# A first part in another order, and two attention spots joined to their neighbours at the end of the second block

## The chip, the core and the metric

The kernel runs on one core of one Trainium2 chip. The metric is the device time of one execution in microseconds (us). Five engines work side by side, each through its own queue in order: TensorE (PE, with PEld for its weight loads), VectorE (DVE), ScalarE (ACT), GpSimd (POOL), and SyncE (SP), which issues the DMAs.

## The reference, cut to what matters

```
out = attention(q, k, v, mem_k, mem_v)     # 4 x 8 heads x 768 x 64; chunks of 32 queries,
                                           # 64 keys each: 16 left, 32 own, 8 right, 8 memory
x   = out as 3072 tokens x 512
h   = x @ w_in                             # 512 -> 2048
g   = s * relu(h)**2 + b
x   = g @ w_out                            # 2048 -> 512
logits = x @ phi                           # 32 slots
slot_in  = softmax(logits over tokens).T @ x
slot_out = relu(slot_in @ w1[e]) @ w2[e]   # 8 experts, 4 slots each
return softmax(logits over slots) @ slot_out
```

## The kernel before

The 3072 tokens are six blocks of 512. Attention is cut into units: one unit is one pair of heads of one block, so a block has four. A unit has three spots on TensorE, with work of other engines between them:

- `att_qk` (line 220): 16 score matmuls of 64x64 into one bank. Then the softmax: on DVE two memsets of masked columns, a maximum (234), a subtraction (235); on ACT the exponential (239); on DVE the sum (247), an added epsilon (248), a reciprocal (249); and a scaling (253), on DVE or, in the first part, on POOL.
- `att_turn` (263): four transposes. `att_half` copies the two halves of the result to a tile `pb`, on ACT (273) or on DVE (275).
- `att_pvmm` (285): 16 value matmuls of 64x64. `att_copy` brings the result to SBUF on ACT (292 or 294), `att_low` forms its low part on DVE (308).

Every large product is done in three matmuls with high and low parts of both operands ("split": the high part by ACT, the low part by DVE or POOL).

Blocks 0 and 1 run in steps n = 0 to 31, sixteen of d_ff for each block. A step has twelve matmuls for h (`mm_h`, 377), then `make_r` (381, ACT), `make_t` (385, DVE), `make_high` (388, ACT), `make_low` (392, DVE), and, one step later, twelve matmuls for y (`mm_y`, 407). The weights arrive as 64-bit words in halves, and each half goes through four operations before it can be used: `w_clamp` (d in the list below, 326), `w_low` (h, 335), `w_high` (e, 330) and `w_end` (E, 340).

The first part, with block 0's attention and all of block 0's steps, follows a list of tokens, `FIRST`: a letter for an operation and a number for the unit, step or half. It sets the order on every engine: B `att_qk`, a maximum and subtraction, b exponential, f sum and reciprocal, j scaling on POOL, U `att_turn`, p and C the two copies to `pb`, V `att_pvmm`, u `att_copy`, X `att_low`, I and i the split of w_in, H and M `mm_h`, z dummy matmuls.

Attention of later units is spread over the steps by the table `bg`. Steps 28 to 31 (`hand_step`) and all that follows up to the tail are in an order written out by hand, which ACT, DVE and POOL keep; PE and SP keep the written order throughout. In a hand step, `tasks` holds the attention spots of the step: a value spot stands ahead of `make_g` (385 to 392), a score or transpose spot behind it.

Blocks 2 and 3 follow in `first_super`, eight rounds p. A round makes seven products (`prod`, 737) into four banks. At its head, bank A (`bank[4]`) takes product a11; ACT copies it out (808, to y0n); product s1 goes to bank C (`bank[6]`); then s2 is added onto what is in A, so PE waits for the copy 808 first. ACT copies C out (826, to y1n), and s4 is added onto C, so PE waits for copy 826. In round 0 both copies stand on ACT's queue behind work of step 31: the split of the operands t2, t3, t4 (651 on ACT, 655 and 665 on DVE) and of the weights w14n, w15n (728 on ACT, 729 on POOL).

Unit 17 is the second of block 4's units; in the kernel before, its scores stand in round 0 between s2 and s4, and its softmax behind s3.

Of the kernel before, what the change touches and what calls it, by code (L numbers as in the profile page):

```python
# [25 lines left out]
KG = 40  # L26
KW = CB * KG + 24
FIRST = (
# [25 lines left out]
def tile_attention_moe_softmoe(  # L54
# [158 lines left out]
    def att_qk(u, b):  # L213
        S = b.rearrange("p (t n) -> p t n", t=8)
        qt, kt = qv(u), kv(u)
        for i in range(4):
            for z in range(2):
                for par in range(2):
                    c = 4 * i + 2 * par + z
                    pe.matmul(S[64 * par:64 * par + 64, 2 * i + z, :], lhsT=qt[:, c].rearrange("p h n -> p (h n)"), rhs=kt[:, KG * c:KG * c + 64],  # L220
                              start=True, stop=True)
# [19 lines left out]
    def att_exp(u, b):  # L241
        att_top(u, b)
        att_e(u)
# [11 lines left out]
    def att_norm(u, last=None):  # L255
        att_sum(u)
        att_mul(u, last or dve)
# [11 lines left out]
    def att_half(u, b, z, fast=True):  # L269
        src = b.rearrange("p (i a h n) -> p i a h n", i=4, a=2, h=2)[64 * z:64 * z + 64]  # L270
        dst = pbv(u)[64 * z:64 * z + 64, :, :, :, z, :]
        if fast:
            act.activation(out=dst, in_=src, func=AF.Copy)  # L273
        else:
            dve.tensor_copy(dst, src)
# [46 lines left out]

    def w_clamp(k):
        hv = half_at[k].rearrange("p (n w) -> p n w", w=2)[:, :, 1]
        eng = dve if k in (0, 1) else pool
        eng.tensor_scalar(out=hv, in0=hv, scalar1=-EXP_TOP, scalar2=EXP_TOP, op0=ALU.max, op1=ALU.min)  # L326

    def w_high(k):
# [243 lines left out]
    for u in range(2 * NHP, 4 * NHP + 1):  # L572
        n0 = NF - 4 + 2 * (u - 2 * NHP)
        bg[n0].append(("qk", u))
        bg[n0 + 2].append(("tr", u))
        bg[n0 + (4 if u < 4 * NHP - 2 else 3)].append(("pv", u))
    for step, task in ((3, "log"), (3, "ytr0"), (5, "etr"), (5, "ytr1"), (7, "ytr2"), (7, "ytr3"), (7, "csoft"), (9, "slot")):
        bg[NF + step].append((task, 0))
    for n, tasks in bg.items():
# [5 lines left out]
    def att_next(a):  # L585
        if a + 2 < NB * NHP:
            load_q(a + 2)
            load_k(a + 2)
# [172 lines left out]
    def first_super(pending):  # L761
# [41 lines left out]
        for p in range(NPR):  # L803
            c11 = hl(ch[0])[:, p % 2]
            more = p + 1 < NPR
            A, D = yq[0], yq[3]
            prod(A, "a11", "b11", p)
            act.activation(out=c11, in_=A, func=AF.Copy)
            if p == 0:
                x_split("t4", 0, 1)  # L810
            if p:
                att_place(4 * NHP + p, D)
                finish(p - 1)
            if p == 1:
                w_split(2, 1)
                evac_spare(yp)
            if p == 5:
                run_bg("csoft", jr)
            if more:
                w_sums(p + 1)  # L820
            w_split(3, p)
            wi_load(p + 2)
            if not more:
                t2_load(0)
            prod(C, "s1", "t1", p)
            act.activation(out=c22, in_=C, func=AF.Copy)
            w_prep(0, p + 1)
            if not more:
                prep(0)
                x_split("b11", 1, 0)  # L830
                x_split("b11", 1, 1)
            prod(A, "s2", "t2", p, False)
            act.activation(out=c12, in_=A, func=AF.Copy)
            w_prep(1, p + 1)
            if not more:
                t2_load(1)
            if p:
                run_bg("pv", 4 * NHP + p, B)
            if more:
                att_qk(4 * NHP + p + 1, D)  # L840
                att_next(4 * NHP + p + 1)
                if p:
                    att_exp(4 * NHP + p + 1, D)
                    att_norm(4 * NHP + p + 1)
            pending.pop(0)()
            if p:
                next_load(p, 0)
            prod(C, "s4", "b22", p, False)
            dve.tensor_tensor(out=c12, in0=C, in1=c12, op=ALU.add)
            if not more:  # L850
                x_sum("t1", 1, 0)
                x_sum("t1", 1, 1)
            prod(A, "s3", "t3", p, False)
            dve.tensor_tensor(out=c22, in0=A, in1=c22, op=ALU.add)  # L854
            if p == 0:
                att_exp(4 * NHP + 1, D)
                att_norm(4 * NHP + 1)

            def square2():
                relu(r2, ch[1])  # L860
                times(cur[G2[p]], ch[1], r2)
                if p:
                    w_prep(2, p + 1)

            if p:
                square2()
            if not more:
                t2_load(4)
                prep(1)
                x_split("t1", 1, 0)  # L870
                x_split("t1", 1, 1)
            late = lambda: None
            for t in routing.get(p, ()):
                if t == "log":
                    late = y_logits(jr, D)
                else:
                    run_bg(t, jr, B if t in ("ytr0", "ytr1", "ytr3") else D)
            pending.pop(0)()
            if p:
                next_load(p, 1)  # L880
            else:
                ws_load(R[3], 1)
            if not more:
                t2_load(6)
                t2_load(7)
            prod(A, "a22", "t4", p, False)
            relu(t21, A)
            times(t21, A, t21)
            late()
            prod(B, "a12", "b21", p)  # L890
            if not more:
                t2_load(5)
            dve.tensor_tensor(out=c11, in0=B, in1=c11, op=ALU.add)
            g_high(t21, G[1])
            relu(t11, c11)
            g_low(t21, G[1])
            times(t11, c11, t11)
            if p == 0:
                square2()
            if more:  # L900
                att_turn(4 * NHP + p + 1, D)
            pending.append(lambda p=p: mm_job(yp, cur[R[(2 * p) % 4]], G[1], p == 0, False))
            pending.append(lambda p=p: mm_job(yp, cur[R[(2 * p + 1) % 4]], G[0], False, p == NPR - 1))
# [327 lines left out]
    with tc.manual_schedule(engines={mybir.EngineType.PE, mybir.EngineType.SP}):  # L1231
# [28 lines left out]
        def took(u, b=None):  # L1260
# [33 lines left out]
            "f": att_sum,  # L1294
            "j": lambda u: att_mul(u, pool),
            "p": lambda u: att_half(u, sbk[u], 0),
            "C": lambda u: att_half(u, sbk[u], 1, u in (0,)),
            "u": lambda u: att_copy(u, sbk[u]),
            "X": lambda u: att_low(u, sbk[u]),
            "Z": w_store,  # L1300
# [32 lines left out]
        def hand_step(n):  # L1333
            m = n - (NSTEP - 4)
            if m == 0:
                split_wi(n + 1)
                wi_load(0)
                wi_load(1)
                ws_load(R[0], NPR, True)
                ws_load(R[1], 0, True)  # L1340
            split_wo(n)
            sp.dma_start(out=DWS[n % NF], in_=WO[n % 2])
            mm_h(n, (0, 1, 2, 3))
            if m == 3:
                w_split(1, 0)
            make_r(n)
            tasks = [lambda t=t, a=a: run_bg(t, a, bank[7] if n == NSTEP - 1 else HB[(n + 1) % 2] if t == "pv" else mbank())
                     for t, a in bg[n]]
            if bg[n][0][0] == "pv":
                tasks.pop(0)()  # L1350
            make_g(n)
            if n + 2 < NSTEP:
                split_wi(n + 2)
            for t in tasks:
                t()
            mm_y(n - 1)
            if m == 0:
                x_sum("t1", 0, 1, pool)
            elif m == 1:
                x_split("t1", 0, 1)  # L1360
            elif m == 2:
                w_sums(0)
                x_sum("t2", 0, 1)
                x_sum("t3", 0, 1)
                x_split("b22", 0, 1)
                w_split(0, 0)
            else:
                x_split("t2", 0, 1)
                x_split("t3", 0, 1)
                x_sum("t4", 0, 1)  # L1370
                w_split(2, 0)
                ws_load(R[2], NPR + 1)
# [258 lines left out]
```

## Time and profile before

| what | us |
|---|---|
| median of three timed runs | 650.23 (649.72 to 650.28) |
| the profiled execution | 649.8 |
| its span, first to last instruction | 648.0 |
| PE busy | 636.5 (98%) |
| DVE, ACT, POOL busy | 441.0, 354.8, 281.2 |

Times in the trace count from the start of the span; the profiled execution lasted 1.8 us longer than its span. PE's mean granted clock was 0.997 of full speed. An engine's busy share is a mean over the whole span; what matters here is the order in which things end in two stretches, the first 26 us and the 12 us from 230 on.

### The profile page before, as it was taken

How to read it: one execution, taken by the hardware profiler on the slowest of the kernel's cores; microseconds unless marked ns; L12 is line 12 of the kernel's file. 1: busy time of each engine (PE TensorE's matmuls, PEld its weight loads, DVE VectorE, ACT ScalarE, POOL GpSimd, SP SyncE). 2: the span in 40 equal slices, each digit the busy share in tenths (PEclk: the TensorE clock that was granted, in tenths of full speed). 3: DMA queues.
4: the chain of work that ended last, by engine and by line, in shares of the span. 5: the costliest groups of instructions: out<-in, count | busy, mean ns of one | idle time of the engine just before them, and what ended most of it. 6: DMA issues, size and time to landing. Idle time of an engine off the chain costs nothing.

```text
span 648.0 us, 12886 instructions
## 1 busy us (share of the span) xinstructions
PE 636.5 (98%) x4965; PEld 511.6 (79%) x4965; DVE 441.0 (68%) x716; ACT 354.8 (55%) x640; POOL 281.2 (43%) x227
## 2 busy tenths in 40 slices
PE   8999999999999999999999999999999999999995
PEld 7788888888878888888788887888887888886384
DVE  6999989666864678656566587616766889676233
ACT  5898887655554556554354555425654456554232
POOL 5897856343333584643534103454455515320000
PEclk9999999999999999999999999999999999999998
DMA  8998854577746755978754687469999789999998
GB/s 331 408 405 306 307 184 171 170 274 252 262 168 212 286 200 211 332 263 297 285 192 180 218 294 227 183 196 379 333 344 323 243 291 334 331 379 409 406 408 323
DMA packets 59821, 183.33 MB, mean 283 GB/s; under 512 B 6640, under 2 KB 7920, under 8 KB 59760
## 3 DMA queue, kind: packets, MB, share of 16 engines
q1 hardware_dynamic: 59760, 182.51, 77.5%
q8 instruction: 39, 0.64, 0.4%
q14 instruction: 22, 0.18, 0.1%
HBM read 136.35 MB, written 46.14 MB: 282 GB/s over the span
## 4 chain that ended last, share of the span: by engine, by line
PE 96%; DVE 2%; ACT 0%; issue 0%; DVEq 0%; POOL 0%; POOLq 0%
PE bank L407 28%; PE bank L737 24%; PE bank L377 13%; PE bank L995 12%; PE bank L285 3%; PE bank L220 3%; PE bank L1486 2%; PE bank L1445 2%; PE bank L459 2%; PE bank L263 2%; PE bank L433 1%; PE bank L475 1%; PE bank L1515 1%; PE bank L1245 1%; PE bank L513 0%
## 5 line engine op out<-in xcount | busy, mean ns | idle before, releaser
L407 PE MATMUL bank<-g,wo 128*128 128x512 f32 x528 | 130.0, 395 | 0.0
L407 PEld LDWEIGHTS bank<-g,wo 128*128 128x128 f32 x528 | 96.9, 188 | 21.7 <-ACT wi L347 0.8
L377 PE MATMUL bank<-x,wi 128*128 128x512 f32 x384 | 92.8, 390 | 0.0
L377 PEld LDWEIGHTS bank<-x,wi 128*128 128x128 f32 x384 | 71.8, 188 | 15.3 <-DVE x L308 0.4
L385 DVE SCALAR_TENSOR_TENSOR rt<-bank,cons,rt 128x512 f32<-128x512 f32 x32 | 23.8, 745 | 29.1 <-ACT rt L381 28.9
L326 POOL TENSOR_SCALAR sp<-sp 128x512 f32<-128x512 f32 x20 | 43.0, 2174 | 0.0
L366 POOL TENSOR_TENSOR wo<-w,wo 128x512 fp32r<-128x512 f32 x16 | 21.9, 1367 | 45.3 <-ACT wo L362 32.5
L729 POOL TENSOR_TENSOR w14n<-sp6n,w14n 128x512 fp32r<-128x512 f32 x8 | 14.5, 1815 | 46.9 <-ACT w14n L728 46.9
L351 POOL TENSOR_TENSOR wi<-w,wi 128x512 fp32r<-128x512 f32 x17 | 22.4, 1318 | 24.8 <-ACT wi L347 21.3
L347 ACT ACTIVATE wi<-w 128x512 fp32r<-128x512 f32 x32 | 20.1, 629 | 19.9 <-PE bank L377 15.0
L392 DVE SCALAR_TENSOR_TENSOR g<-rt,cons,g 128x512 fp32r<-128x512 f32 x32 | 25.6, 799 | 6.2 <-ACT g L388 5.9
L362 ACT ACTIVATE wo<-w 128x512 fp32r<-128x512 f32 x32 | 20.1, 627 | 16.4 <-PE bank L407 9.0
L285 PEld LDWEIGHTS bank<-pb,v 128*64 128x64 f32 x704 | 22.2, 138 | 8.0 <-issue 2.5
L388 ACT ACTIVATE g<-rt,cons 128x512 fp32r<-128x512 f32 x32 | 23.1, 720 | 9.0 <-DVE rt L385 8.5
L239 ACT ACTIVATE ep<-ep 128x512 f32<-128x512 f32 x22 | 13.9, 632 | 23.1 <-DVE ep L235 23.0
L285 PE MATMUL bank<-pb,v 128*64 128x64 f32 x704 | 25.1, 225 | 0.8 <-ACT pb L273 0.5
L220 PE MATMUL bank<-k,q 128*64 128x64 f32 x704 | 24.8, 226 | 0.0
L752 ACT ACTIVATE rt1n<-y1n 128x1024 f32<-128x1024 f32 x8 | 8.5, 1058 | 29.0 <-DVE y1n L854 29.0
L220 PEld LDWEIGHTS bank<-k,q 128*64 128x64 f32 x704 | 22.9, 141 | 1.4 <-issue 1.3
L381 ACT ACTIVATE rt<-bank 128x512 f32<-128x512 f32 x32 | 18.7, 583 | 6.3 <-PE bank L377 6.1
L985 POOL TENSOR_TENSOR k0n<-sp5n,k0n 128x512 fp32r<-128x512 f32 x6 | 8.2, 1360 | 30.4 <-ACT k0n L984 30.3
L247 DVE TENSOR_REDUCE ast<-ep 128x8 f32<-128x512 f32 x22 | 15.0, 681 | 8.6 <-ACT ep L239 8.2
(696 smaller groups left out, 1742.4 us busy)
## 6 DMA issues: line engine op xcount, KB each, us to landing
v<-vd SPq DMA_DIRECT2D x22, 512.0 KB, 5.1
sp<-wd SPq DMA_DIRECT2D x22, 512.0 KB, 9.3
q<-qd SPq DMA_DIRECT2D x20, 512.0 KB, 7.3
dws<-wo SPq DMA_DIRECT2D x16, 512.0 KB, 6.3
k<-kd SPq DMA_DIRECT2D x22, 332.0 KB, 7.0
wo<-dws SPq DMA_DIRECT2D x12, 512.0 KB, 4.5
dwi<-w SPq DMA_DIRECT2D x16, 256.0 KB, 6.5
dwr<-w SPq DMA_DIRECT2D x16, 256.0 KB, 6.3
```

The source lines that it names most:

```text
L220: pe.matmul(S[64 * par:64 * par + 64, 2 * i + z, :], lhsT=qt[:, c].rearrange("p h n -> p (h n)"), rhs=kt[:, KG * c:KG * c + 64], start=Tru ...
L285: pe.matmul(b[64 * h:64 * h + 64, 64 * m:64 * m + 64], lhsT=vt[:, m, h, :], rhs=pb[:, m // 2, m % 2, h].rearrange("p z n -> p (z n)"), sta ...
L326: eng.tensor_scalar(out=hv, in0=hv, scalar1=-EXP_TOP, scalar2=EXP_TOP, op0=ALU.max, op1=ALU.min)
L351: (dve if n < NF and n not in (0,) else pool).tensor_tensor(out=r32(t[:, 1]), in0=raw, in1=t[:, 0], op=ALU.subtract)
L366: (dve if n < NF else pool).tensor_tensor(out=r32(t[:, :, 1]), in0=raw, in1=t[:, :, 0], op=ALU.subtract)
L377: pe.matmul(HB[n % 2], lhsT=r32(w[:, a, kt, :]), rhs=r32(x[:, b]), start=(kt == 0 and i == 0), stop=(kt == 3 and i == 2))
L385: dve.scalar_tensor_tensor(out=t, in0=HB[n % 2], scalar=s_col, in1=r, op0=ALU.mult, op1=ALU.mult)
L388: act.activation(out=r32(hl(G[n % 2])[:, 0]), in_=hl(RT[n % 2])[:, 1], func=AF.Identity, bias=b_col)
L392: dve.scalar_tensor_tensor(out=r32(g[:, 1]), in0=t, scalar=b_col, in1=g[:, 0], op0=ALU.add, op1=ALU.subtract)
L407: pe.matmul(yb[dt], lhsT=r32(w[:, dt // 2, a, dt % 2 * 128:dt % 2 * 128 + 128]), rhs=r32(g[:, b]), start=(first and i == 0), stop=(last an ...
L737: pe.matmul(b, lhsT=r32(wv[:, a, kt, :]), rhs=r32(xv[:, c]), start=(first and kt == 0 and i == 0), stop=(kt == 1 and i == 2), skip_group_c ...
L995: pe.matmul(banks[d], lhsT=r32(w[:, a, d * 128:d * 128 + 128]), rhs=r32(g[:, b]), start=(first and i == 0), stop=(last and i == 2), skip_g ...
```

## The change

It has four parts.

1. The head of `FIRST` is rewritten. Units 0 to 3 keep their sequence on PE, but of the copies to `pb`, C1 and C3 go from DVE to ACT; `w_low` and `w_high` of weight half 0 go to other places on ACT; tiles for weight halves are handed out in another order further on.
2. `w_clamp` of half 0 goes from DVE to POOL.
3. The value spot of unit 14 goes from step 27 to step 28.
4. The scores of unit 17 and their whole softmax go from round 0 of `first_super` to step 31, behind the value spot of unit 16 and ahead of `make_g(31)`.

```diff
-    "q0 k0 q1 k1 K0 q2 k2 q3 k3 v0 w1 v1 v2 v3 w3 z8 S0 s0 B0 S1 s1 a0 B1 S2 s2 b0 B2 a1 S3 s3 f0 b1 B3 "
...
+    "q0 k0 q1 k1 K0 q2 k2 q3 k3 v0 w1 v1 v2 v3 w3 z8 S0 s0 S1 s1 B0 a0 B1 S2 s2 a1 z2 B2 b0 f0 S3 s3 a2 "
+    "b1 B3 f1 j0 k4 w1 a3 K1 z4 b2 h0 q4 w2 U0 d0 p0 z5 C0 e0 b3 j1 f2 V0 U1 u0 p1 j2 f3 C1 U2 p2 E0 C2 "
...
     def w_clamp(k):
...
-        eng = dve if k in (0, 1) else pool
+        eng = dve if k in (1,) else pool
...
-        bg[n0 + (4 if u < 4 * NHP - 2 else 3)].append(("pv", u))
+        bg[n0 + (4 if u < 4 * NHP - 1 else 3)].append(("pv", u))
...
             if p:
                 run_bg("pv", 4 * NHP + p, B)
-            if more:
-                att_qk(4 * NHP + p + 1, D)
-                att_next(4 * NHP + p + 1)
-                if p:
-                    att_exp(4 * NHP + p + 1, D)
-                    att_norm(4 * NHP + p + 1)
+            if more and p:
+                run_bg("qk", 4 * NHP + p + 1, D)
...
-            if p == 0:
-                att_exp(4 * NHP + 1, D)
-                att_norm(4 * NHP + 1)
...
-            "C": lambda u: att_half(u, sbk[u], 1, u in (0,)),
+            "C": lambda u: att_half(u, sbk[u], 1, u in (0, 1, 3)),
...
             if bg[n][0][0] == "pv":
                 tasks.pop(0)()
+            if m == 3:
+                run_bg("qk", 4 * NHP + 1, bank[6])
             make_g(n)
```

The first place is PE at the end of block 1: the difference in steps 28 and 31 and in round 0 (285 value matmuls, 220 scores, 263 transposes, 407 y, 737 products).

```order
 L377 MATMUL bank_195<-x_93,wi_83 128x512 x3
 L377 MATMUL bank_195<-x_94,wi_83 128x512 x3
+L285 MATMUL bank_196<-pb_105,v_103 64x64 x16
 L220 MATMUL bank_197<-k_101,q_99 64x64 x16
 L263 MATMUL bank_198<-cons,ep 128x128 x4
@@ -549,4 +549,5 @@
 L377 MATMUL bank_196<-x_94,wi_84 128x512 x3
 L285 MATMUL bank_198<-pb_105,v_103 64x64 x16
+L220 MATMUL bank_197<-k_102,q_100 64x64 x16
 L407 MATMUL bank_191<-g_95,wo_85 128x512
```

Unit 14's values now stand directly ahead of unit 16's scores, and unit 17's scores directly behind unit 16's values.

The second place is ACT's queue at the same point, after the change: from `make_r(31)` (381) to the copy of bank C (826).

```order
L381 ACTIVATE rt_98<-bank_196 128x512
L294 ACTIVATE x00n<-bank_198 128x512
L239 ACTIVATE ep<-ep 128x512
L388 ACTIVATE g_96<-rt_98,cons 128x512
L651 ACTIVATE w11n<-x01n 128x512
L651 ACTIVATE w12n<-x01n 128x512
L728 ACTIVATE w14n<-sp6n 128x512
L808 ACTIVATE y0n<-bank_195 128x512
L651 ACTIVATE w13n<-x01n 128x512
L728 ACTIVATE w15n<-sp4n 128x512
L826 ACTIVATE y1n<-bank_197 128x512
```

Before, the row of line 239 stood much later, behind the copies 808, 826 and 833; the others stood in this same order.

The third place is DVE's queue there, after the change: from the low part of t3's first half (655, w10n) on.

```order
L655 TENSOR_TENSOR w10n<-x03n,w10n 128x512
L233 MEMSET bank_197 64x8
L231 MEMSET bank_197 64x16
L234 TENSOR_REDUCE ast_188<-bank_197 128x8
L235 TENSOR_TENSOR ep<-bank_197,ast_188 128x512
L247 TENSOR_REDUCE ast_188<-ep 128x8
L248 TENSOR_SCALAR ast_188<-ast_188 128x8
L249 RECIPROCAL ast_188<-ast_188 128x8
L253 TENSOR_TENSOR ep<-ep,ast_188 128x512
L385 SCALAR_TENSOR_TENSOR rt_98<-bank_196,cons,rt_98 128x512
L392 SCALAR_TENSOR_TENSOR g_96<-rt_98,cons,g_96 128x512
```

Before, 385 came directly behind w10n, and the eight rows of the softmax stood further on, behind the two additions onto y1n (849, 854).

## Rows read from the trace of the kernel before

**Rows 1.** The page: busy time and share of each engine.

```profile
PE 636.5 (98%) x4965; PEld 511.6 (79%) x4965; DVE 441.0 (68%) x716; ACT 354.8 (55%) x640; POOL 281.2 (43%) x227
```

**Rows 2.** Waits of PE, total, times, longest in us; the longest of nine.

```profile
PE bank L1245 <- POOL w L1241: 1.3, 1, 1.3
```

**Rows 3.** The chain of waits: start, us, engine, line, instructions.

```profile
195.55 1.08 PE bank L285 x32
196.64 0.93 PE bank L220 x32
...
231.25 2.94 PE bank L407 x12
234.19 4.08 PE bank L737 x18
238.27 1.08 PE bank L220 x32
239.36 2.95 PE bank L737 x12
242.30 2.72 PE bank L407 x12
```

**Rows 4.** DVE's timeline, 230 to 248 us: start, us, line, operation.

```profile
231.64 0.75 DVE L385 SCALAR_TENSOR_TENSOR rt<-bank,cons,rt 128x512 f32<-128x512 f32 x1
...
235.06 1.78 DVE L665 TENSOR_TENSOR x01n<-x03n,x01n 128x512 f32<-128x512 f32 x1
...
243.10 0.07 DVE L233 MEMSET bank<- 64x8 f32 x1
...
247.23 0.74 DVE L755 SCALAR_TENSOR_TENSOR rt0n<-bank,cons,rt0n 128x512 f32<-128x512 f32 x1
```

**Rows 5.** ACT's timeline, 230 to 241 us.

```profile
232.43 0.72 ACT L388 ACTIVATE g<-rt,cons 128x512 fp32r<-128x512 f32 x1 [0.53 <-DVE rt L385]
...
234.10 0.62 ACT L728 ACTIVATE w14n<-sp6n 128x512 fp32r<-128x512 f32 x1
235.59 0.60 ACT L808 ACTIVATE y0n<-bank 128x512 f32<-128x512 f32 x1 [0.88 <-PE bank L737]
...
237.93 0.58 ACT L826 ACTIVATE y1n<-bank 128x512 f32<-128x512 f32 x1
```

**Rows 6.** DVE's timeline, 12 to 26 us.

```profile
15.97 0.38 DVE L326 TENSOR_SCALAR sp<-sp 128x512 f32<-128x512 f32 x1
...
17.55 0.69 DVE L275 COPY pb<-bank 64x512 f32<-64x512 f32 x1
18.28 0.98 DVE L340 SCALAR_TENSOR_TENSOR w<-sp 128x512 uint32<-128x512 uint32 x1
...
24.51 0.68 DVE L308 TENSOR_TENSOR x<-bank,x 128x512 fp32r<-128x512 f32 x1
```

**Rows 7.** POOL's timeline, 10 to 40 us.

```profile
13.64 1.04 POOL L253 TENSOR_TENSOR ep<-ep,ast 128x512 f32<-128x512 f32 x1 [1.49 <-ACT pb L273]
16.20 1.06 POOL L253 TENSOR_TENSOR rt<-rt,ast 128x512 f32<-128x512 f32 x1 [1.51 <-DVE ast L249]
...
21.25 10.99 POOL L326 TENSOR_SCALAR sp<-sp 128x512 f32<-128x512 f32 x5
```

**Rows 8.** PE's timeline, 12 to 32 us.

```profile
17.31 0.66 PE L263 MATMUL bank<-cons,rt 128*128 128x128 f32 x4 [0.18 <-POOL rt L253]
18.30 1.15 PE L285 MATMUL bank<-pb,v 128*64 128x64 f32 x32 [0.33 <-DVE pb L275]
...
22.35 1.15 PE L285 MATMUL bank<-pb,yt 128*64 128x64 f32 x32 [0.26 <-DVE pb L275]
```

**Rows 9.** Instructions on the tile of weight halves, 5 to 20 us: issues, and landing times.

```profile
L320 SPq DMA_DIRECT2D sp<-wd x7: 327/328/436, 5.5 to 18.8; - x7
...
DMA to landing us min/median/max: 7.0/10.3/11.4
```

**Rows 10.** Stretches: busy us of each engine, granted clock, DMA share, GB/s.

```profile
644.00:648.00 4.00, 0.00 (x0) 0.00 (x0) 0.00 (x0) 0.00 (x0) 0.00 (x0) 0.58 0.63 252
```

5 rows, old and new, of the table FIRST are left out of this document.

## Prediction

> **What bounds the kernel now.** I read the page first, then PE's waits, then the chain that ended last, then the timelines of the two stretches that the change touches. The page shows PE busy for 636.5 us [rows 1]; the list of waits has nine for PE, together 5.5 us, the longest 1.3 us at the very start [rows 2], and all of them lie in the first 23 us or behind 596 us. Between these the kernel costs what PE's instructions cost. So a gain has to be PE work that vanishes or a start that comes earlier, and a wait that the change makes inside this stretch is paid in full: nothing later can absorb it. DVE, ACT and POOL are ahead of PE there, and the question for each edit is by how much.
>
> **Two joins.** A lone spot of 64x64 matmuls takes 1.08 us, and the group of twelve wide matmuls behind it takes 2.95 instead of 2.72: 1.08 + 0.23 = 1.31 us. A spot directly behind another one takes 0.93 [rows 3]. Unit 17's scores stood alone (at 238.27) and will stand behind unit 16's values: 1.31 - 0.93 = 0.38 saved. Unit 14's values stood alone with the same two durations, and will stand ahead of unit 16's scores, which then lose the 0.15 of a first spot, while the 0.23 behind the values goes: 0.38 again. Together 0.75 us.
>
> **What unit 17's softmax does in step 31.** This is the part that decides. All times here are those of the trace of before, with the y group of step 30 as the anchor. That group began at 231.25 [rows 3]; now unit 17's scores stand ahead of it, so they end at 231.25 + 0.93 = 232.18. DVE's queue has the softmax next, ahead of line 385. In round 0 the same eight operations took from 243.10 to 247.23, with the exponential of ACT in the middle: 4.13 us [rows 4]. So 385, which started at 231.64, starts at 232.18 + 4.13 = 236.31, which is 4.67 later. Behind it on ACT stand, in order, 388, the high parts of w11n and w12n, w14n, and only then the copy 808 of bank A. From the start of 385 the row of 388 begins 0.79 later and that of w14n ends 3.08 later [rows 4, 5]; 808 would follow at once and takes 0.60, and since neighbours on ACT overlap by about 0.1, it ends 3.6 after 385: at 239.9. Before, it ended at 236.19 and waited for PE, not PE for it.
>
> PE meanwhile does the y group (2.94, to 235.12) and then a11 and s1, twelve of the 18 matmuls that took 4.08, hence 2.72: s2 is due at 237.84 [rows 3]. It adds onto bank A and must have 808 behind it. Wait one: 239.9 - 237.84 = 2.1 us.
>
> s2 is six matmuls, 1.36, and ends at 241.3. Then s4 adds onto bank C and needs the copy 826. That copy ended at 237.93 + 0.58 = 238.51 [rows 5], which is 6.87 after the start of 385, and ACT and DVE between the two had no slack: 665 starts 3.42 and ends 5.20 after 385 [rows 4], and then ACT has w13n, w15n and 826 in a row. So 826 ends at 236.31 + 6.87 = 243.2, and wait two is 1.9 us. In the kernel before s2 ended at 238.27, ahead of 238.51 too; unit 17's scores, which stood there, covered that difference [rows 3]. The change takes the cover away and makes the copy 4.67 later. Sum of both waits: 4.0 us. Bank C itself is free in time for s1: even the whole softmax ends (236.31) before s1 is due (236.48).
>
> Bounds: 665 took 1.78 beside a working POOL, and a similar operation took 0.68 [rows 4, 6]. If POOL is not beside it this time, wait two shrinks by 1.1, and the sum is 2.9. If one operation of the softmax is stretched as much, the sum is 5.1. I take 4.0, since POOL's work there hangs on the same ACT row (w14n) and so moves along.
>
> Unit 14's values hold nothing up: their bank is next needed by `mm_h(29)`, behind a y group of 2.7 us, and their copy on ACT falls into a time in which ACT waits for 385.
>
> **The head.** DVE's queue loses a clamp of 0.38 and two copies of 0.69 with their gaps, 18.28 - 17.55 = 0.73 each [rows 6]. POOL gains the clamp, at 10.99 / 5 = 2.2 us [rows 7]. Half 0 was issued at 5.5 and had the shortest landing, 7.0, so it lands at 12.5 [rows 9]; POOL is idle from 13.64 - 1.49 = 12.15 on, and the clamp runs from about 12.65 to 14.85. That pushes unit 1's scaling from 13.64 to 14.9, so to 15.95, just ahead of unit 2's at 16.20, which stays [rows 7]. Unit 1's turn on PE comes at 16.0 and its two copies, both on ACT now, end at 16.6 + 1.2 = 17.8. Unit 2's turn is still at 17.31 and holds PE for 0.65, so unit 1's values start at 17.95, not 18.30 [rows 8]. From there PE has work without a gap, if the others keep up: values 1.08, turn 3 0.59, values 2 1.08, the first three wide matmuls 0.68, so the values of unit 3 start at 21.4 instead of 22.35 [rows 8]. DVE does keep up: the recombination of half 0 (340) starts at about 17.35 instead of 18.28 (less one copy, 0.73, and part of the clamp), after which ACT and POOL have the low part of w_in at about 20.6. C3 on ACT ends at 21.4. After the values of unit 3 come u3 on ACT and 308 on DVE, which I get at 23.6 instead of 24.51 [rows 6]: 0.9 us earlier, and so is all that follows. Bounds: if the clamp takes 2.5, the exponential of unit 3 behind it on ACT is late for DVE and 0.4 is left; the PE chain allows no more than 1.0.
>
> One row speaks to the price of the clamp: on DVE it took 0.38 at 15.97, when POOL was idle [rows 6, 7]. [...]
>
> **Sum.** 4.0 - 0.75 - 0.9 = +2.35 us. The profiled execution took 649.8 and would take 652.15; the median of before is 650.23, 0.4 above it, so I forecast 652.6.
>
> **Rivals.**
> - *Not slower: the copies come in time* (0.12). One mechanism: 385 and the ACT rows behind it get through before s2 is due. Then joins and head remain: 650.23 - 1.65 = 648.6. It takes 808 ending by 237.84, hence 385 starting by 234.25, hence a softmax of 2.1 us instead of 4.13. Nothing in rows 4 speaks for that, except that the walk needs every operation to queue as the order prints it.
> - *One wait only* (0.13). 808 is late, but 826 is not, because w13n and w15n are quicker: 650.23 + 2.1 - 1.65 = 650.7. It takes 826 ending by 241.3, 5.0 after 385, against 6.87 in the rows.
> - *The head gives nothing* (0.10): the clamp on POOL is longer or DVE stretches beside it. 650.23 + 4.0 - 0.75 = 653.5. For it: DVE's 340 took 0.98 at 18.28 [rows 6], with POOL at work.
> - *The granted clock falls* (0.05). [...]
> - *My sum* holds with 0.60.
>
> **Numbers.** A measurement of this kernel tells about 0.2%, 1.3 us, from no change. The sum's own range: waits of 2.9 with a head of 1.0 give 651.4, waits of 5.1 with a head of 0.4 give 654.2. With the one-wait rival and short of the two on the outside, the range is 650.7 to 654.0. Faster by over 0.2%: 0.12, the first rival. Within 0.2%, up to 651.5: 0.13 for one wait and 0.05 from the low end of the sum. Slower: 0.70.
>
> **What would show it.** In the profile after, PE's waits should name ACT's 808 with about 2.1 us and ACT's 826 with about 1.9, both near 237 to 243; DVE's 385 of step 31 should stand behind a 253; the values of unit 3 should start near 21.4 instead of 22.35; the joined spots should read 1.08 and 0.93. I am wrong if PE shows no wait there, or if DVE's 385 starts within 2 us of the scores' end.

## The result and the profile after

| | before | after |
|---|---|---|
| median, us | 649.98 (six runs, 648.59 to 650.28) | 653.56 (six runs, 652.6 to 654.97) |
| ratio, 95% interval | | 1.0057 [1.0046, 1.0068] |
| profiled execution, its span | 649.8, 648.0 | 653.7, 651.9 |

The change costs about 3.6 us, 0.6%: slower, as forecast, and inside the range, though 1.2 more than the sum's +2.35. PE's list of waits (total, times, longest) has two new entries, both inside the stretch that had none [rows 2]:

```profile
PE bank L737 <- ACT y0n L808: 2.2, 1, 2.2
...
PE bank L737 <- ACT y1n L826: 0.4, 1, 0.4
```

and the page has PE busier by 1.4 us than [rows 1], at the same 4965 instructions:

```profile
PE 637.9 (98%) x4965; PEld 512.5 (79%) x4965; DVE 439.9 (67%) x713; ACT 355.7 (55%) x642; POOL 282.7 (43%) x228
```

PE's timeline from 230 us on (start, us, line; in brackets the wait ahead of the row and who ended it):

```profile
229.68 1.15 PE L285 MATMUL bank<-pb,v 128*64 128x64 f32 x32
230.66 1.10 PE L220 MATMUL bank<-k,q 128*64 128x64 f32 x32
231.69 3.02 PE L407 MATMUL bank<-g,wo 128*128 128x512 f32 x12
...
236.59 0.84 PE L737 MATMUL bank<-w9n,wi1n 128*128 128x512 f32 x3
239.58 1.65 PE L737 MATMUL bank<-w4n,wi1n 128*128 128x512 f32 x3 [2.15 <-ACT y0n L808]
241.03 1.48 PE L737 MATMUL bank<-w11n,wi1n 128*128 128x512 f32 x3
242.88 0.95 PE L737 MATMUL bank<-w3n,w14n 128*128 128x512 f32 x3 [0.38 <-ACT y1n L826]
243.67 0.84 PE L737 MATMUL bank<-w10n,w14n 128*128 128x512 f32 x3
```

The joined spots take 231.69 - 229.68 = 2.01, which is the 1.08 and 0.93 of the forecast. s2 is the pair w4n, w11n; s4 is w3n, w10n. Wait one is 2.15. Wait two reads 0.38 instead of 1.9, but look at the durations: s2's groups of three take 1.65 and 1.48 instead of 0.84. PE was at half its clock, 0.50. By stretches (length, busy us of PE, PEld, DVE, ACT, POOL, then the granted clock):

```profile
238.00:239.00 1.00, 0.00 (x0) 0.00 (x0) 1.00 (x3) 1.00 (x4) 0.00 (x0) 1.00 0.65 258
...
240.00:241.00 1.00, 1.00 (x3) 0.74 (x3) 1.00 (x1) 0.00 (x0) 1.00 (x2) 0.50 0.00 0
241.00:242.00 1.00, 1.00 (x4) 0.66 (x2) 0.25 (x2) 0.80 (x2) 0.92 (x2) 0.50 0.55 225
242.00:243.00 1.00, 0.62 (x3) 0.12 (x2) 1.00 (x1) 1.00 (x3) 0.92 (x2) 0.54 1.21 320
```

So s2 lasted from 239.58 to 242.88 - 0.38 = 242.50, 2.92 instead of 1.36, and ran while copy 826 was still being waited for: 2.15 + 1.56 + 0.38 = 4.09 us of loss in all, against 4.0 in the sum. In the stretch from 238 to 239, while PE waited, the clock was still 1.00; at 240 it was 0.50. DVE shows what is late; compare [rows 4]:

```profile
231.85 0.07 DVE L233 MEMSET bank<- 64x8 f32 x1 [0.83 <-PE bank L220]
...
235.38 0.69 DVE L253 TENSOR_TENSOR ep<-ep,ast 128x512 f32<-128x512 f32 x1
235.98 0.75 DVE L385 SCALAR_TENSOR_TENSOR rt<-bank,cons,rt 128x512 f32<-128x512 f32 x1
...
239.39 1.77 DVE L665 TENSOR_TENSOR x01n<-x03n,x01n 128x512 f32<-128x512 f32 x1
```

385 starts 235.98 - 231.85 = 4.13 behind the softmax's first row, the 4.13 of the sum. ACT's timeline [rows 5] hands it on:

```profile
236.76 0.72 ACT L388 ACTIVATE g<-rt,cons 128x512 fp32r<-128x512 f32 x1 [2.59 <-DVE rt L385]
...
238.43 0.61 ACT L728 ACTIVATE w14n<-sp6n 128x512 fp32r<-128x512 f32 x1
238.95 0.57 ACT L808 ACTIVATE y0n<-bank 128x512 f32<-128x512 f32 x1
241.20 0.63 ACT L651 ACTIVATE w13n<-x01n 128x512 fp32r<-128x512 f32 x1 [1.67 <-DVE x01n L665]
...
242.25 0.58 ACT L826 ACTIVATE y1n<-bank 128x512 f32<-128x512 f32 x1
```

808 ends 239.52, 3.54 behind 385's start (3.6 in the sum); 826 ends 242.83, 6.85 behind it (6.87).

The chain shows PE's restart for s4 and s3:

```profile
242.88 2.99 PE bank L737 x12
245.88 2.72 PE bank L407 x12
```

Before it read 2.95 behind the lone scores [rows 3]. The stop cost these groups what the lone spot did, so the 0.23 of that join never came.

At the head, PE's timeline [rows 8]:

```profile
17.93 0.66 PE L263 MATMUL bank<-cons,rt 128*128 128x128 f32 x4 [0.80 <-POOL rt L253]
...
22.26 1.15 PE L285 MATMUL bank<-pb,yt 128*64 128x64 f32 x32
```

The values of unit 3 start at 22.26, not 21.4 (22.35 before): the head's 0.9 is missing.

### The profile page after: what moved, and what is told of

It reads as the page before. It is cut to its first block, busy times and chain, and to the rows that moved or that the text cites. A ratio compares the mean times of both kernels' runs of the same rounds, so it can differ in the third digit from the quotient of the medians.

```text
span 651.9 us, 12882 instructions
## 1 busy us (share of the span) xinstructions
PE 637.9 (98%) x4965; PEld 512.5 (79%) x4965; DVE 439.9 (67%) x713; ACT 355.7 (55%) x642; POOL 282.7 (43%) x228
## 4 chain that ended last, share of the span: by engine, by line
PE 61%; DVE 0%; issue 0%; ACT 0%; DVEq 0%
PE bank L737 23%; PE bank L407 14%; PE bank L987 12%; PE bank L1480 2%; PE bank L1439 2%; PE bank L459 1%; PE bank L285 1%; PE bank L1509 1%; PE bank L220 1%; PE bank L433 1%; PE bank L475 1%; PE bank L513 0%; PE bank L263 0%; PE bank L1458 0%; PE bank L1496 0%
## 5 line engine op out<-in xcount | busy, mean ns | idle before, releaser
L326 POOL TENSOR_SCALAR sp<-sp 128x512 f32<-128x512 f32 x21 | 44.8, 2156 | 1.0 <-DMA sp<-wd 1.0
```

## Experiments

**The head alone, twice.**

```diff
-    "q0 k0 q1 k1 K0 q2 k2 q3 k3 v0 w1 v1 v2 v3 w3 z8 S0 s0 B0 S1 s1 a0 B1 S2 s2 b0 B2 a1 S3 s3 f0 b1 B3 "
...
+    "q0 k0 q1 k1 K0 q2 k2 q3 k3 v0 w1 v1 v2 v3 w3 z8 S0 s0 S1 s1 B0 a0 B1 S2 s2 a1 z2 B2 b0 f0 S3 s3 a2 "
...
-        eng = dve if k in (0, 1) else pool
+        eng = dve if k in (1,) else pool
-            "C": lambda u: att_half(u, sbk[u], 1, u in (0,)),
+            "C": lambda u: att_half(u, sbk[u], 1, u in (0, 1, 3)),
```

The new list also puts the dummy matmuls (z) in other places; the head was tried as a whole, and which of its edits gives or takes what is not shown, apart from what follows.

> The kernel before with the new head alone (the list, the clamp of half 0 on POOL, the copies C1 and C3 on ACT); both joins undone. My sum: 0.9 us faster than before, with the values of unit 3 near 21.4 us instead of 22.35. Rival, the head gives nothing (what the trace of the changed kernel suggests): within 0.1 us of before, the values of unit 3 at 22.2 to 22.4, because a transfer and POOL's scaling of unit 2 come later and DVE's second copy waits for ACT instead of standing in DVE's own queue.

> The kernel before with the new head alone, once more. In its first profile the values of unit 3 began at 21.43 us (22.35 before: my 0.9), but its median was only 0.2 us below. If the head's 0.9 is steady: 0.6 to 1.1 faster than before, values of unit 3 again 0.6 to 1.0 ahead of the old head's 22.0 to 22.5. If it hangs on when the first transfers land: 0 to 0.4 faster, with values of unit 3 later than 21.8.

Measured 649.59 and 649.53 against 649.8 and 649.89: ratios 0.9996 [0.9985, 1.0007] and 0.9996 [0.9987, 1.0004]. So 0.3 us by the ratio in both, with 1 inside both intervals: nearer to nothing than to 0.9, though the first trace has unit 3's values at 21.43. That number misleads: in this execution DVE's softmax began earlier too. Taken from DVE's second memset (line 231, at 8.39 before), the four traces with the old head agree within 0.01 us: unit 3's values start 13.96 behind it (13.97 in one). With the new head:

| trace | memset | clamp starts on POOL, behind it | longest row 248 of units 1 and 2 | unit 3's values, behind it |
|---|---|---|---|---|
| head alone, second | 8.60 | 3.82 | 0.17 | 13.24 |
| late softmax and head | 8.47 | 4.42 | 0.40 | 13.46 |
| t4 behind | 8.49 | 4.45 | 0.41 | 13.49 |
| head alone, first | 7.85 | 4.72 | 0.50 | 13.58 |
| changed kernel | 8.60 | 4.81 | 0.58 | 13.66 |

The head gives 13.96 - 13.24 = 0.72 where POOL's clamp comes early, and 0.30 in the changed kernel's trace, whose memset was 0.21 later besides. POOL and then DVE there:

```profile
13.41 2.00 POOL L326 TENSOR_SCALAR sp<-sp 128x512 f32<-128x512 f32 x1 [1.04 <-DMA sp<-wd]
15.38 1.03 POOL L253 TENSOR_TENSOR ep<-ep,ast 128x512 f32<-128x512 f32 x1
```

```profile
15.87 0.58 DVE L248 TENSOR_SCALAR ast<-ast 128x8 f32<-128x8 f32 x1
16.48 0.20 DVE L249 RECIPROCAL ast<-ast 128x8 f32<-128x8 f32 x1
```

and in the second run of the head alone, in the same order:

```profile
12.42 1.99 POOL L326 TENSOR_SCALAR sp<-sp 128x512 f32<-128x512 f32 x1
14.37 1.04 POOL L253 TENSOR_TENSOR ep<-ep,ast 128x512 f32<-128x512 f32 x1
```

```profile
13.31 0.17 DVE L248 TENSOR_SCALAR ast<-ast 128x8 f32<-128x8 f32 x1
...
15.86 0.17 DVE L248 TENSOR_SCALAR ast<-ast 128x8 f32<-128x8 f32 x1
16.07 0.20 DVE L249 RECIPROCAL ast<-ast 128x8 f32<-128x8 f32 x1
```

Half 0's transfer lands late, POOL's clamp waits 1.04 for it, unit 1's scaling ends at 16.41 instead of 15.41, and DVE's tiny row 248, at the same time in both, doesn't end before it: 0.58 instead of 0.17. Unit 2's scaling hangs on it. In each trace of the table the loss against 13.24 is the stretch of a row 248 within 0.01 us (0.58 - 0.17 = 0.41 against 0.42; 0.33 against 0.34; 0.23 against 0.22), and so it is in two later traces (0.55 with 13.62, the softmax behind 385 to 392 a second time; 0.51 with 13.57, t4 behind as well). In "late softmax and head" and "t4 behind" it is the row of unit 1, beside the clamp itself. That POOL works beside it is not enough: in the second run of the head unit 1's row, at 13.31, lies inside the clamp (12.42 to 14.41) and takes its 0.17. In "late softmax and head" it came 0.28 us behind the clamp's start and took 0.40; why the one and not the other is not shown. The remaining 0.2 between 0.72 and 0.9 is in PE's timeline of the second run:

```profile
20.90 0.96 PE L377 MATMUL bank<-x,wi 128*128 128x512 f32 x3
21.84 1.15 PE L285 MATMUL bank<-pb,yt 128*64 128x64 f32 x32
```

The three wide matmuls behind a spot take 21.84 - 20.90 = 0.94, not 0.68: about the 0.23 that the sum booked for the joins and left out here.

**The load of half 0 one place earlier**, with the head alone:

```diff
-    "q0 k0 q1 k1 K0 q2 k2 q3 k3 v0 w1 v1 v2 v3 w3 z8 S0 s0 S1 s1 B0 a0 B1 S2 s2 a1 z2 B2 b0 f0 S3 s3 a2 "
+    "q0 k0 q1 k1 K0 q2 k2 q3 k3 w1 v0 v1 v2 v3 w3 z8 S0 s0 S1 s1 B0 a0 B1 S2 s2 a1 z2 B2 b0 f0 S3 s3 a2 "
```

> The kernel before with the new head alone, and the load of weight half 0 issued one place earlier on SP, ahead of the first value load. My reading: the head gives 0.7 where POOL's clamp of half 0 starts without waiting for its transfer (3.8 us behind DVE's second memset), and less the later the transfer lands; with the earlier load the clamp never waits, so POOL shows no wait there, the values of unit 3 start 13.2 us behind that memset (13.96 with the old head), and the time is 0.7 us below before. Rival, the landing is not what takes the gain: 0.2 to 0.4 below before, as for the head alone.

Measured 648.85 against 650.08, ratio 0.9986 [0.9978, 0.9995], so 0.9 us by the ratio and 1.2 by the medians. POOL and PE:

```profile
11.70 2.00 POOL L326 TENSOR_SCALAR sp<-sp 128x512 f32<-128x512 f32 x1
```

```profile
21.21 1.15 PE L285 MATMUL bank<-pb,yt 128*64 128x64 f32 x32
```

The clamp waits for nothing, 3.74 behind the memset at 7.96, and unit 3's values come 13.25 behind it. The offsets decide; the times agree, though their interval still meets that of the head alone.

**Both spots, old head.**

```diff
-    "q0 k0 q1 k1 K0 q2 k2 q3 k3 v0 w1 v1 v2 v3 w3 z8 S0 s0 S1 s1 B0 a0 B1 S2 s2 a1 z2 B2 b0 f0 S3 s3 a2 "
...
+    "q0 k0 q1 k1 K0 q2 k2 q3 k3 v0 w1 v1 v2 v3 w3 z8 S0 s0 B0 S1 s1 a0 B1 S2 s2 b0 B2 a1 S3 s3 f0 b1 B3 "
...
-        eng = dve if k in (1,) else pool
+        eng = dve if k in (0, 1) else pool
...
-            "C": lambda u: att_half(u, sbk[u], 1, u in (0, 1, 3)),
+            "C": lambda u: att_half(u, sbk[u], 1, u in (0,)),
```

> The changed kernel with the old head: both spots moved, nothing else. My sum: waits of 4.0 less two joins of 0.38 each, so 3.25 us slower than before. With the restart of PE 0.27 us behind each stop, as in the trace of the changed kernel: 3.5. If the head gives its 0.9 after all, this kernel is 0.9 slower than the changed one; if the head gives nothing, the two are equal within 0.1. The theory that the waits are not the cause: no more than 1 us slower than before.

Measured 653.36 against 649.8, ratio 1.0058 [1.0046, 1.007], 3.6 us: the spots are the whole loss. PE's timeline:

```profile
239.32 0.96 PE L737 MATMUL bank<-w4n,wi1n 128*128 128x512 f32 x3 [2.15 <-ACT y0n L808]
240.12 0.85 PE L737 MATMUL bank<-w11n,wi1n 128*128 128x512 f32 x3
242.62 0.96 PE L737 MATMUL bank<-w3n,w14n 128*128 128x512 f32 x3 [1.65 <-ACT y1n L826]
```

Here the clock held (1.00 from 240 to 244). s2 took 1.65 with its restart, 0.29 more than 1.36, and wait two is 1.65: 2.15 + 0.29 + 1.65 = 4.09, the same loss as in the changed kernel's trace. What the half clock took there, wait two gave back.

**Unit 14's values alone**, and **both joins with the softmax left where it was**: the first edit is the first pair of lines, the second is all of them.

```diff
-        bg[n0 + (4 if u < 4 * NHP - 2 else 3)].append(("pv", u))
+        bg[n0 + (4 if u < 4 * NHP - 1 else 3)].append(("pv", u))
...
+            if m == 3:
+                att_qk(4 * NHP + 1, bank[7])
+                att_next(4 * NHP + 1)
             make_g(n)
```

(In the second, unit 16's values take `HB[0]`, and `first_super` loses only the scores of unit 17: it keeps `att_exp` and `att_norm` behind s3.)

> The kernel before with unit 14's values at step 28 and nothing else. My sum: 0.38 us faster than before, no new wait of PE. Rival: the bank or the copy of these values holds something up, and the kernel is 0 to 0.5 us slower, with a wait of PE near 204 us.

> The kernel before with both joins (unit 14's values at step 28; unit 17's scores directly behind unit 16's values in step 31, the scores in bank 7, the values in the bank of h that is free), but unit 17's softmax stays where it was, in round 0 behind s3. If the softmax ahead of line 385 is the whole cause of the waits: the wait on copy 808 is gone, the wait on copy 826 is 0.24 us (cover of the score spot is gone, the copy itself is not later), so 0.75 less 0.24: 0.5 us faster than before. Rival, the place of the scores on PE is the cause: waits of 1 us or more on the copies remain and the kernel is slower than before.

Measured 649.43 and 648.98 against 649.8: ratios 0.9994 [0.9985, 1.0003] and 0.9989 [0.998, 0.9997]. The first is not clear of noise by its time; the traces show more. The chain of the kernel before had, at the first spot of step 31:

```profile
230.17 1.08 PE bank L285 x32
```

and that of the second edit:

```profile
229.81 1.08 PE bank L285 x32
230.89 0.93 PE bank L220 x32
231.82 2.95 PE bank L407 x12
234.77 6.80 PE bank L737 x30
241.57 2.72 PE bank L407 x12
```

Unit 3's values start 0.01 us apart in these two traces (22.36 and 22.35), so their times can be compared. The first spot comes at 229.81 instead of 230.17: 0.36 for unit 14's join. From there to the y group behind the products it is 11.76 instead of 12.13 [rows 3]: 0.37 for unit 17's. Both joins are worth their 0.38, and thirty products run without a stop: the scores' place on PE costs nothing. The 0.24 that I expected on 826 isn't there; joined scores still delay s2 by their 0.93, so that cover was not lost (826 ends at 238.29, s4 is due at 238.69). It is the softmax ahead of 385 that makes the copies late.

**t4 behind copy 826**, in the changed kernel:

```diff
-            if p == 0:
-                x_split("t4", 0, 1)
...
             act.activation(out=c22, in_=C, func=AF.Copy)
+            if p == 0:
+                x_split("t4", 0, 1)
```

> The changed kernel, but in round 0 the high part of t4's second half (651 to w13n) stands on ACT behind the copy 826 and not ahead of copy and w15n, so that 826 no longer hangs on DVE's 665. My sum, the two waits are separate terms: wait one stays at 2.1, wait two (1.65 in the run with both spots alone) goes, 1.7 us less than the changed kernel, about 1.9 slower than before. Rival, the half clock seen behind wait one in the changed kernel's trace is a steady cost that wait two covered: s2 then takes 2.9 instead of 1.4 and the kernel is only 0.2 to 0.4 faster than the changed one, 3.3 slower than before.

Measured 652.4 (651.37 to 653.0) against 649.89, ratio 1.0037 [1.0025, 1.0049], 2.4 us over before: between my 1.9 and the rival's 3.3, so the time alone does not decide. The profiled execution took 651.37.

```profile
239.31 0.96 PE L737 MATMUL bank<-w4n,wi1n 128*128 128x512 f32 x3 [2.15 <-ACT y0n L808]
240.11 0.85 PE L737 MATMUL bank<-w11n,wi1n 128*128 128x512 f32 x3
240.80 0.84 PE L737 MATMUL bank<-w3n,w14n 128*128 128x512 f32 x3
```

Wait two is gone and s4 follows at once; the two waits are separate terms. The half clock did not come in this trace (1.00 from 236 to 244), so it is no steady cost of a 2.15 us wait. The mean granted clocks of the five executions suggest that it came in three of them: 0.998 with 651.37 and 651.81, 0.996 with 652.4 to 653.0. Where these three lost their time is not shown, since only one execution has a trace.

**The softmax behind 385 to 392**, twice, and **with t4 behind 826 as well** (the edit above added):

```diff
-                run_bg("qk", 4 * NHP + 1, bank[6])
+                att_qk(4 * NHP + 1, bank[6])
+                att_next(4 * NHP + 1)
             make_g(n)
+            if m == 3:
+                att_exp(4 * NHP + 1, bank[6])
+                att_norm(4 * NHP + 1)
```

> The changed kernel with unit 17's softmax behind lines 385, 388 and 392 of step 31 instead of ahead of them. My reading: DVE's 665 and with it copy 826 are as late as before the edit, and only wait one shrinks, from 2.1 to about 0.5 (the three high parts and 808 stand behind the exponential on ACT); wait two takes over what wait one loses, about 3.3, and the time is that of the changed kernel within 0.4 us. Rival, wait one is a cost of its own: 1.6 us faster than the changed kernel.

> The kernel with unit 17's softmax behind lines 385 to 392, once more: its first profile was of an execution 4 us above its median. The waits of 0.4, 0.3 and 3.2 us, less joins and head, make 3.4 us over before; 5.6 were measured. If the half clock behind the long wait is the missing 2 us, a profile near 655.5 shows PE at half its clock for 4 to 5.5 us behind the wait on copy 826, and a head without a fall. If not: no half clock there, and the 2 us stand in other waits.

> The kernel with unit 17's softmax behind lines 385 to 392 (which took 5.6 us more than before, with a wait of 3.2 on copy 826 and then 5.3 us of PE at half its clock) and with t4's high part behind copy 826 as well. My reading: the 2 us that the softmax behind the lines cost beyond my sum are the half clock behind the long wait. Without that wait there is no fall: two short waits remain (copy 808, 0.4, and w11n's low part, 0.3), the joins and the head give 1.1, and the kernel is within 0.5 us of before. Rival, the extra 2 us come from the order of DVE's rows: 2 us slower than before.

The softmax behind the lines measured 655.47 and 655.24 in its two runs, against 649.89 and 650.23: ratios 1.01 [1.0081, 1.0119] and 1.0075 [1.0061, 1.0089]. Neither theory of mine: the waits did change places (0.4, 0.3 and 3.2), but the kernel got slower than the changed one. The second run's profiled execution, 656.06, shows why, on PE and by stretch:

```profile
242.68 1.65 PE L737 MATMUL bank<-w3n,w14n 128*128 128x512 f32 x3 [3.20 <-ACT y1n L826]
244.12 1.48 PE L737 MATMUL bank<-w10n,w14n 128*128 128x512 f32 x3
245.40 1.48 PE L737 MATMUL bank<-w5n,w14n 128*128 128x512 f32 x3
246.68 1.42 PE L737 MATMUL bank<-w12n,w14n 128*128 128x512 f32 x3
247.94 2.92 PE L407 MATMUL bank<-g,wo 128*128 128x512 f32 x12
```

```profile
244.00:246.00 2.00, 2.00 (x6) 1.51 (x6) 0.29 (x1) 0.00 (x0) 1.83 (x2) 0.50 0.65 236
```

Behind a wait of 3.20, at a clock of 0.50, twelve matmuls take 247.94 - 242.68 = 5.26 instead of 2.72: 2.5 us, with no later wait to hide it. The first run's trace has the same rows (a wait of 3.21 and 1.65, 1.48, 1.48, 1.48). It is of an execution of 659.62 us, 4.2 above its median, and is the worst case of the head: half 0 landed later still (POOL's clamp waited 2.02 us for it, until 14.20), ACT has `w_low` (335) of that half ahead of the copies to `pb`, PE stood 1.95 us for such a copy (273) and ran at 0.50 of its clock from 18 to 20 us, and unit 3's values came 15.13 behind the memset. So that loss is not the stretched row 248 alone.

With t4 behind 826 too, 651.87 against 650.08, ratio 1.0029 [1.0019, 1.0038], 1.9 us over before, where I had expected 0.5 at most. No three products took over 0.98 in its trace from 226 to 256, against 1.42 to 1.65 at half clock, but there is a third wait:

```profile
242.56 0.98 PE L737 MATMUL bank<-w5n,w14n 128*128 128x512 f32 x3 [1.62 <-ACT y1n L833]
```

s3 needs copy 833, which still stood on ACT behind w13n and so behind DVE's 665. Waits of 0.4, 0.3 and 1.6 are 2.4, and three restarts at 0.27 each (2.99 against 2.72 in the changed kernel's chain) 0.8; less 1.1 for joins and head, that is 2.1. So the rival had the time, and part of the cause: the third wait comes from DVE's order, with 665 behind the softmax. The half clock explains the first form of this kernel, not what is left here.

**A better version**: the changed kernel with unit 17's softmax back in round 0 (unit 16's values take `HB[0]` again); then with the early load of half 0 as well.

```diff
             if m == 3:
-                run_bg("qk", 4 * NHP + 1, bank[6])
+                att_qk(4 * NHP + 1, bank[7])
+                att_next(4 * NHP + 1)
...
+            if p == 0:
+                att_exp(4 * NHP + 1, D)
+                att_norm(4 * NHP + 1)
```

> The changed kernel with unit 17's softmax put back into round 0 behind s3, its scores kept behind unit 16's values (in bank 7, the values in a free bank of h): new head and both joins, no long softmax ahead of line 385. Joins measured 0.8 us faster than before without the head. If the head gives its 0.9: 1.7 us faster than before, the values of unit 3 near 21.4 to 21.8 us. If the head gives nothing: 0.8 faster. No wait of PE on copies 808 and 826 near 240 us by either.

> Both joins with unit 17's softmax in round 0, the new head, and the early load of half 0. The same without the early load was 1.1 us faster than before. If the landing of half 0 takes part of the head's gain: 1.4 to 1.6 faster. If not: 1.1 again.

Measured 648.79 against 649.89, ratio 0.9985 [0.9976, 0.9994], and 648.78 against 650.08, ratio 0.9979 [0.9971, 0.9988]: 1.1 and 1.3 us by the medians, both faster than either kernel. The second falls short of my 1.4 to 1.6, by less than its interval. That the early load adds to it is in the trace (13.25 behind the memset instead of 13.46); the intervals overlap.

## Why the prediction held, and where its sum was off

- **Waits (4.0): right in place and size.** 4.09 in the changed kernel's trace and in that of both spots alone, with s2's slower run counted. Lines, order and offsets are those forecast: 385 behind 4.13 us of softmax, 808 3.54 and 826 6.85 behind it. Only "the change takes the cover away" is wrong: with the softmax left in round 0 no wait on 826 came.
- **Joins (0.75): mis-sized, 0.5.** Unit 14's is worth 0.36. Of unit 17's, only 1.08 - 0.93 = 0.15 came: the wait ahead of s4 makes its restart as long as the lone spot did (2.99 against 2.95).
- **The head (0.9): mis-sized, 0.3 on the trace's own clock, and 0.09 against the trace of before.** Two steps of its sum failed. "The first three wide matmuls 0.68" takes 0.94. And unit 2's scaling, which "stays" in the sum, stayed in the second run of the head (7.82 behind the memset, 7.81 before) but came 8.22 behind it in the changed kernel's trace, where row 248 took 0.58: that row is 0.17 alone, 0.40 to 0.58 where it was stretched in the traces of the table. That DVE's softmax rows keep their times beside the clamp was my assumption; counted from the memset no trace shows the 0.9 that needs it, and those of the table give 0.30 to 0.72. The 128x512 rows of the softmax did stay at 0.67 to 0.69, and inside the second run's clamp row 248 took its 0.17. Larger rows stretched elsewhere: 665 takes 1.77 beside POOL (239.39 to 241.16 in the changed kernel's trace, where POOL was busy throughout), and w11n's 655 took 0.69 at 238.19 there, with POOL idle, but 1.77 at 236.99 with the softmax and t4 both behind. POOL's 729 starts 0.08 behind the end of ACT's w14n in the changed kernel's trace (239.12 and 239.04); with w14n ending at 236.75, I estimate that it was at work from 236.83 on. My own bounds had 665's 1.78. So the rival "the head gives nothing" was right about the time (653.5) and about DVE stretching, though not about 340, which took 0.64 at 18.05.
- **The granted clock.** I gave its fall 0.05. It did fall in the changed kernel's trace, to 0.50, but cost almost nothing there, since s2 ran slowly (2.92 instead of 1.36) inside a wait that was there anyway. Where no wait followed, behind 3.2 us, it cost 2.5. Over the six executions the lower mean clocks go with the longer times (0.997 and 0.998: 652.6 to 653.4; 0.992 to 0.995: 653.7 to 655.0), and the means of the two groups are 1.1 us apart. Whether the half clock is what separates them is not shown, since only one of the six has a trace.
- **Not settled.** Why a 2.15 us wait brings the half clock in one trace (0.50 from 240 to 242) and not in two others (1.00 from 240 to 244) is not shown.

Added up against before: 4.09 for the waits, less 0.51 for the joins and 0.09 for the head (22.26 against 22.35), is 3.5. The y group behind s3 starts 245.88 - 242.30 = 3.58 later, and the medians say 3.6. (The two profiled executions are 3.9 apart; the last 0.3 lies behind this stretch.)

So direction and mechanism held by the reasoning. That 653.56 still lies inside the range is partly luck: its upper end rested on waits of 5.1 us, which did not come, and it took in what joins and head failed to give.

## What to carry to other kernels

Here a join saved the few tenths that its row showed when the other engines' part of the joined spot stayed where it was; the other two places tried for the softmax made the kernel 1.9 to 5.6 us slower than before. So move the matmuls, and leave the softmax behind the rows that PE waits for soonest. Before an operation goes to another engine, ask what that engine must now wait for ahead of the rows behind it: the clamp put a transfer ahead of two scalings, and issuing that transfer one place earlier took the wait away. When removing one wait, follow the engine's queue to the next copy behind the same late row (808, then 826, then 833).

## Not expected of the hardware

- A 128x8 operation on DVE of 0.17 us took 0.40 to 0.58 beside some 128x512 ones on POOL; beside a scaling it ended as that did (16.45 and 16.41 in the changed kernel's trace). Inside a clamp it could also take its 0.17 (13.31 in the second run of the head).
- Behind a stop of 2.15 us PE ran at half its clock (0.50) in one of three traces, behind 3.2 us in both, through 2.9 and 5.3 us of matmuls; in one trace a stop of 1.95 us in the head was followed by it too.
